# Weight sums of the second layer on GpSimd, earlier in the program; high parts of weights in two operations

## The chip, the cores and the metric

The kernel runs on one core of a Trainium2 chip. The metric is the device time of one execution in microseconds (us). Engines are called as in the profile: PE (TensorE, matmuls), PEld (its weight loads), DVE (VectorE), ACT (ScalarE), POOL (GpSimd), SP (SyncE, which here issues the large DMAs). A name with a q behind it (DVEq) is an engine's queue of instructions, where it takes branches and waits on semaphores. L832 is line 832 of the kernel before.

## The reference, cut to what matters

A Nyström attention is followed by two mixture-of-experts layers with one expert for each token. The second layer, in which all of the change lies, is this:

```python
logits = x @ w_gate + modality_bias[modality_id]
e_idx = np.argmax(logits, axis=1)
...
for e in range(E):                      # E = 8
    mask = e_idx == e
    if not mask.any():
        continue
    h = np.maximum(x[mask] @ w1[e], 0.0)          # 512 -> 1024
    out[mask] = gate_w[mask, None] * (h @ w2[e])  # 1024 -> 512
```

There are 4608 tokens. All is float32 outside; inside, a matrix is split into a float16 high part and a float16 rest, and a product is three float16 matmuls.

## The kernel before

The attention runs over 8 batches in an order written out by hand, with the first tiles of the first layer in its gaps. Then come three stretches: a loop over the first layer's tiles of 128 tokens; three tiles that stand outside of any loop (called "last", "out1" and "out2" by their plans, and first, second and third tile below); and a loop over the second layer in which one step handles two tiles of 128 tokens (`pair`). With the given inputs that loop has 17 steps. What is said of steps below counts them from 1 at the loop's start.

**A step.** Matmuls of `w1` first (L1402, 96 of them), then seven products with `w2` (L1429, 84 matmuls). The seven products are Strassen's scheme in Winograd's form: sums of blocks of the activations (`s`, on DVE, L1358 to L1370), and sums of blocks of `w2`. The sums of `w2` depend on the weights alone and are made once for each half of an expert's `w2`: `mix` (L825) writes four differences of 128x512 float32 into `tf`; `mix_hi` (L836, ACT) writes their float16 high part `wth`; `mix_lo` (L841, DVE, two operations) writes the rest `wtl`. So the chain for one half is four operations on `tf`, one on ACT, two on DVE.

**New weights.** While one expert is computed, the next expert's weights arrive in four pieces and are split: `split_hi` (L813, ACT) makes the high part `whi`, `split_lo` and `split_lo2` (L818, DVE) the rest `wlo`. A number in a table, `word`, says for a step whether a piece is split (`word > 7`) and whether it is a piece of `w2`, so that its sums are made too (`word > 11`). Each such part stands in an `If` on `word` in the step's code; it is taken in 4 of the 17 steps, and the sums in two of these, steps 7 and 8.

**What sets the order.** Each engine works through its own queue in the order in which the code issues. Where the parts of a step stand is set by a table, `PLANS`: a number is the matmul group behind which the parts are issued (for `pair`, 0 to 7 are the groups of `w1`, 8 to 14 the seven products; -1 is the head of the step). In `pair` of before, `s0` is `split_hi`, `s1` and `s2` are the two halves of the rest, `s3` is the four sums and `mix_hi`, `s4` is `mix_lo`. `f0` and `f1` (L1355) and `g0` and `g1` (L1364) make the activations' sums; ACT's `sh` of L1367 in `g1` is what the third product's later matmuls read. `u1` to `u4`, `y22`, `y21` and `y12` add the products.

**The three tiles.** They make the sums of the first expert of the second layer: the first tile those of one half (`mixa`, `mix0` to `mix2`), the third tile those of the other (`mixb`, `mix3` to `mix5`), from `again`, a second copy of that half of `w2`, which lies in the buffer `s` of the activations' sums. While the second tile runs, DVE also works out the table of the loop (`tile_table`, some 90 tiny operations, L903 to L1033) in two parts: the first stands ahead of the second tile's operations in DVE's queue, the second ahead of the third tile's. From that table SP reads which rows of tokens to load for the loop's first step (`xab`, L1084, two transposing DMAs).

**The loop's entry.** PE's first matmul of the loop waits for both of these loads, and for DVE and ACT to have come to the loop. SP's first issue of a step is the load of the next weights' piece into `stg` (L791); in step 1 it, too, waits until DVE has come to the loop.

## Time and profile before

| | |
|---|---|
| median of 3 runs | 1017.72 us (1017.53 to 1018.48) |
| profiled execution | 1013.91 us, span of its instructions 1012.2 us |
| PE busy | 964.6 us, 95% of the span |
| DVE, ACT, POOL busy | 720.7, 426.0, 228.8 us (71%, 42%, 23%) |
| mean granted TensorE clock | 0.984 |
| chain that ended last | its last 2 us: output rows (L1244, L1253) |

The profiled execution and the timed runs are different executions; the profiled one has 3.8 us less than the median. PE is busy nearly throughout, so a stretch is read by PE's idle time in it and by what ended that idle time. A matmul's row covers its latency too: in the loop each starts some 0.11 us behind the one before it and is shown as 0.27 us, so that a stall shows shorter than it is. The length of a step is best taken from one step's first matmul of L1402 to the next step's.

### The profile page before, as it was taken

To read this page: it belongs to the slowest core of one execution; us is meant where nothing else is said; L and a number is where in the kernel's file an instruction comes from. 1 tells how busy PE (TensorE), PEld (TensorE's weight loads), DVE (VectorE), ACT (ScalarE), POOL (GpSimd) and SP (SyncE) were. 2 spreads that over 40 slices of the span, in tenths; PEclk is the share of its full clock that TensorE was granted. 3 is DMA by queue.
4 is the path that set the end of the run, shared out by engine and by line. 5 is a ranking of instruction groups with operands and counts; after the bars stand their busy time and mean duration, and the time that the engine had idled before them with its cause. 6 is when DMAs were issued, how large, how long until landed. Compare 5 with 4: busy or idle time off the path is not lost. (4 is left out here: it accounts for less than half of the span.)

```text
span 1012.2 us, 36241 instructions
## 1 busy us (share of the span) xinstructions
PE 964.6 (95%) x11663; PEld 737.2 (73%) x11664; DVE 720.7 (71%) x2708; ACT 426.0 (42%) x993; POOL 228.8 (23%) x311
## 2 busy tenths in 40 slices
PE   6989998989899999999999999989999999999997
PEld 3655554656677777777767767768888888888886
DVE  6888878958777877877877777855466676545644
ACT  3565756832233433433433433333343444333332
POOL 6476766445010010010010010111100110010011
PEclk9998979989999999999999999999999999999999
DMA  8557587265565462265562345531212121221212
GB/s 281 192 184 257 181 280 291 75 226 142 117 167 157 126 183 65 66 166 156 131 183 66 72 127 148 129 98 34 63 42 63 43 59 48 61 59 46 63 44 62
DMA packets 166419, 125.31 MB, mean 124 GB/s; under 512 B 137662, under 2 KB 137662, under 8 KB 165328
## 3 DMA queue, kind: packets, MB, share of 16 engines
q1 hardware_dynamic: 155536, 95.42, 35.8%
q0 software_dynamic: 9088, 28.95, 7.5%
q8 instruction: 41, 0.67, 0.3%
q10 hardware_dynamic: 1728, 0.06, 0.1%
q14 instruction: 26, 0.21, 0.1%
HBM read 60.48 MB, written 34.83 MB: 94 GB/s over the span
## 5 line engine op out<-in xcount | busy, mean ns | idle before, releaser
L1285 PE MATMUL b_hp<-xl,whi 128*128 128x128 f16 x2368 | 204.1, 219 | 1.2 <-DMA xl<-reg 1.2
L1285 PE MATMUL b_hp<-xl,wlo 128*128 128x128 f16 x1184 | 201.9, 219 | 0.0
L1285 PEld LDWEIGHTS <-whi 128*128 128x128 f16 x2624 | 199.7, 98 | 2.6 <-issue 1.6
L1402 PE MATMUL b_hp<-xab,whi 128*128 128x256 f16 x1088 | 179.1, 273 | 1.2 <-DVEq L1453 1.2
L1402 PE MATMUL b_hp<-xab,wlo 128*128 128x256 f16 x544 | 148.3, 273 | 0.0
L1285 PEld LDWEIGHTS <-wlo 128*128 128x128 f16 x1312 | 128.5, 98 | 0.1
L1336 PE MATMUL ybank<-wlo,hh 128*128 128x512 f16 x328 | 124.6, 380 | 1.0 <-DVE wlo L809 1.0
L1336 PE MATMUL ybank<-whi,hh 128*128 128x512 f16 x328 | 124.6, 380 | 0.0
L1336 PE MATMUL ybank<-whi,hl 128*128 128x512 f16 x328 | 122.3, 380 | 0.0
L1223 POOL DMA_INDIRECT reg<-rows,si x38 | 37.4, 985 | 359.6 <-DVE rr L1154 338.5
L1402 PEld LDWEIGHTS <-whi 128*128 128x128 f16 x1088 | 106.3, 98 | 14.0 <-ACTq L1453 1.7
L1146 ACT ACTIVATE rt<-ybank,sc 128x512 f16<-128x512 f32 x38 | 26.1, 687 | 211.5 <-DVE off L1568 193.9
L1336 PEld LDWEIGHTS <-hh 128*128 128x128 f16 x656 | 62.1, 98 | 67.0 <-issue 0.5
L818 DVE SCALAR_TENSOR_TENSOR wlo<-stg,whi x76 | 92.7, 1220 | 20.3 <-issue 10.9
L1244 POOL DMA_INDIRECT out_dram<-osbb,tokb x18 | 18.5, 1030 | 294.4 <-DVEq L1517 213.4
L813 ACT ACTIVATE whi<-stg x38 | 72.3, 1903 | 0.0
L1358 DVE SCALAR_TENSOR_TENSOR s<-b_hp,r 128x256 f32<-128x256 f32 x34 | 14.4, 424 | 78.5 <-ACT r L1357 69.2
L1130 DVE TENSOR_REDUCE sc<-ybank 128x1 f32<-128x512 f32 x38 | 26.3, 691 | 56.6 <-PE L1285 49.4
L1293 ACT ACTIVATE hh<-b_hp 128x512 f16<-128x512 f32 x74 | 44.1, 597 | 48.1 <-PE b_hp L1285 28.3
L1336 PEld LDWEIGHTS <-hl 128*128 128x128 f16 x328 | 32.1, 98 | 40.1 <-issue 1.6
L1429 PEld LDWEIGHTS <-sh 128*128 128x128 f16 x544 | 53.0, 98 | 9.8 <-ACT sh L1367 3.8
L1402 PEld LDWEIGHTS <-wlo 128*128 128x128 f16 x544 | 53.2, 98 | 6.2
(437 smaller groups left out, 2149.7 us busy)
## 6 DMA issues: line engine op xcount, KB each, us to landing
stg<-in_wall_dram SPq DMA_DIRECT2D x29, 1024.0 KB, 5.5
kq<-in_qk_dram SPq DMA_DIRECT2D x32, 576.0 KB, 6.2
v<-in_v_dram SPq DMA_DIRECT2D x8, 1024.0 KB, 8.2
reg<-zrow SPq DMA_DIRECT2D x18, 264.0 KB, 8.6
v<-in_v_dram SPq DMA_DIRECT2D x8, 128.0 KB, 8.2
s<-in_wall_dram SPq DMA_DIRECT2D x1, 1024.0 KB, 6.7
xl<-reg SPq DMA_TRANSPOSE x41, 3.3
mt<-reg SPq DMA_DIRECT2D x41, 8.0 KB, 4.3
```

Of the source, the lines that this page charges most:

```text
L813: return self.tc.nc.scalar.activation(self.slot(self.ws[d].hi, i), self.slot(self.stg, i), AF.Copy, scale=WS)
L818: return self.tc.nc.vector.scalar_tensor_tensor(self.slot(w.lo, i, a), self.slot(self.stg, i, a), WS, self.slot(w.hi, i, a), op0=ALU.mult, ...
L1130: v.tensor_reduce(sc[:, 0:1], y, axis=AX.X, op=ALU.max, apply_absolute_value=True)
L1146: a.activation(rt[:, 0:DM], y, AF.Copy, scale=sc[:, 1:2])
L1223: w = nc.gpsimd.indirect_dma_start(out=k.reg[:, :], out_offset=bass.IndirectOffsetOnAxis(ap=self.si.bitcast(U32), axis=0), in_=rows, in_of ...
L1244: return nc.gpsimd.indirect_dma_start(out=self.out[:, :], out_offset=bass.IndirectOffsetOnAxis(ap=tok.bitcast(U32), axis=0), in_=osb, in_o ...
L1285: mm = nc.tensor.matmul(hp[ft // 4][:, ft % 4], lhsT=ww[c][:, ft * P:(ft + 1) * P], rhs=self.xl[:, x], start=n == 0, stop=n == 11)
L1293: self.read[i] = [nc.scalar.activation(hh[:, 4 * i:4 * i + 4], hp[i], AF.Relu)]
L1336: nc.tensor.matmul(self.y, lhsT=a[:, ft], rhs=ww[ft], start=n == 0, stop=n == 23)
L1358: v.scalar_tensor_tensor(s[:, 2, c], h[:, :, 0], 0.0, r21[:, c], op0=ALU.max, op1=ALU.subtract)
L1402: nc.tensor.matmul(hp[ft // 2][:, ft % 2], lhsT=ww[c][:, ft * P:(ft + 1) * P], rhs=self.xab[:, x], start=n == 0, stop=n == 11)
L1429: nc.tensor.matmul(bank[:, half[0]], lhsT=l[:, c], rhs=r[c], start=new and c == 0 and i == 0, stop=c == 3 and i == 2, skip_group_check=not ...
```

## The change

All sums but those of `mixa` (first tile) go from DVE to POOL. In a step they move from `s3` (behind the third product) to a part of their own, `add`, at the head of the step, behind the first group of `w1`; `s3` keeps `mix_hi`. Outside of the loop, `mixb` and `mix3` move from the third tile to the second, and `mix4` and `mix5` into the third tile's groups of `w1`. `split_hi` of the second layer becomes two operations of half the size, the second of which (`hi2`) stands three groups later. POOL reads `word` too, so that every `If` on it is now a branch for POOL as well; `add` and `hi2` are two more of them for ACT and DVE.

```diff
-    def split_hi(self, d, i):
-        return self.tc.nc.scalar.activation(self.slot(self.ws[d].hi, i), self.slot(self.stg, i), AF.Copy, scale=WS)
+    def split_hi(self, d, i, a=slice(0, 2)):
+        return self.tc.nc.scalar.activation(self.slot(self.ws[d].hi, i, a), self.slot(self.stg, i, a), AF.Copy, scale=WS)
...
-    def mix(self, v, k):
+    def mix(self, v, k, eng=None):
...
-        return self.tc.nc.vector.tensor_tensor(o, x, y, op=ALU.subtract)
+        return (eng or self.tc.nc.vector).tensor_tensor(o, x, y, op=ALU.subtract)
...
-    "out1": {-1: "out load", 3: "hh0 hl0", 7: "after1 hh1 hl1", 9: "told"},
-    "out2": {-1: "out load", 3: "hh0 hl0", 7: "after1 hh1 hl1 told", 9: "mixb mix3 mix4 mix5", 15: "rest"},
-    "pair": {-1: "out load", 0: "s0", 1: "f0 s1", 3: "f1", 5: "g0", 7: "after1 g1 s2 told", 8: "u1",
+    "out1": {-1: "out load", 3: "hh0 hl0", 7: "after1 hh1 hl1", 9: "told mixb mix3"},
+    "out2": {-1: "out load", 3: "hh0 hl0 mix4", 7: "after1 hh1 hl1 told mix5", 15: "rest"},
+    "pair": {-1: "out load", 0: "s0 add", 1: "f0 s1", 3: "f1 hi2", 5: "g0", 7: "after1 g1 s2 told", 8: "u1",
              10: "u2 u3 s3", 11: "y22 u4", 12: "y21 outb", 13: "y12 s4"},
...
-                word = field(i, CUT, 15, (ET.Activation, ET.DVE))
+                word = field(i, CUT, 15, (ET.Activation, ET.DVE, ET.Pool))
...
+                if layer:
+                    hi = [lambda d, i, a=a: wts.split_hi(d, i, a) for a in range(2)]
+                    return [part(f) for f in (*hi, wts.split_lo, wts.split_lo2)]
                 return [part(f) for f in (wts.split_hi, wts.split_lo, wts.split_lo2)]
...
-                        r = wts.mix(wts.slot(wts.stg, cut), n)
+                        r = wts.mix(wts.slot(wts.stg, cut), n, nc.gpsimd)
...
-                return dict(s0=when(7, hi), s1=when(7, lo), s2=when(7, lo2), s3=when(11, m["mixa"], m["mix0"]),
+                return dict(s0=when(7, hi), s1=when(7, lo), hi2=when(7, hi2), s2=when(7, lo2), add=when(11, m["mixa"]), s3=when(11, m["mix0"]),
                             s4=when(11, m["mix1"], m["mix2"]))
...
-        def add(v):
+        def add(v, eng=None):
             for i in range(4):
-                wts.mix(v, i)
+                wts.mix(v, i, eng)
...
-                   mix2=lambda: wts.mix_lo(p, 1, 1), mixb=lambda: add(again), mix3=lambda: wts.mix_hi(p, 0),
+                   mix2=lambda: wts.mix_lo(p, 1, 1), mixb=lambda: add(again, nc.gpsimd), mix3=lambda: wts.mix_hi(p, 0),
```

The second tile on POOL, before: the rows of output (L1244) in each of the two arms that the tile has for the two sets of weights, and nothing else.

```order
L1750 COMPARE_AND_BRANCH
L1244 DMA out_dram<-osb,tok 4608x512
L1750 UNCONDITIONAL_BRANCH
L1244 DMA out_dram<-osb,tok 4608x512
L1750 UNCONDITIONAL_BRANCH
L847 TENSOR_LOAD numi
```

The same place of the changed kernel (its lines from 1488 on have numbers up to 3 higher):

```order
L1753 COMPARE_AND_BRANCH
L1244 DMA out_dram<-osb,tok 4608x512
L832 TENSOR_TENSOR tf<-s 128x512 x2
L832 TENSOR_TENSOR tf<-s,tf 128x512
L832 TENSOR_TENSOR tf<-tf,s 128x512
L1753 UNCONDITIONAL_BRANCH
```

The four sums stand directly behind the output rows of the first tile, so POOL can start them while DVE works on the table's first part. The third tile on DVE, before, in one arm: the rests of the hidden layer (`hl`), then the four sums and the two operations of `wtl`.

```order
L1296 SCALAR_TENSOR_TENSOR hl<-b_hp_4929,hh 128x512
L1296 SCALAR_TENSOR_TENSOR hl<-b_hp_4930,hh 128x512
L1237 TENSOR_SCALAR mul<-mt 128x1
L1238 COPY tok<-mt 128x1
L832 TENSOR_TENSOR tf<-s 128x512 x2
L832 TENSOR_TENSOR tf<-s,tf 128x512
L832 TENSOR_TENSOR tf<-tf,s 128x512
L841 SCALAR_TENSOR_TENSOR wtl_4906<-tf,wth_4905 128x1024 x2
```

And now:

```order
L1296 SCALAR_TENSOR_TENSOR hl<-b_hp_4929,hh 128x512
L841 SCALAR_TENSOR_TENSOR wtl_4906<-tf,wth_4905 128x1024
L1296 SCALAR_TENSOR_TENSOR hl<-b_hp_4930,hh 128x512
L1237 TENSOR_SCALAR mul<-mt 128x1
L1238 COPY tok<-mt 128x1
L841 SCALAR_TENSOR_TENSOR wtl_4906<-tf,wth_4905 128x1024
```

The sums are gone, and the two operations of `wtl` stand behind one `hl` each. The head of a step on POOL in the changed kernel (register operations of the last two sums left out): the two issues of output rows, the `If` of `s0`, which is empty for POOL, and that of `add`.

```order
L1244 DMA out_dram<-osbb,tokb 4608x512
L1244 REGISTER_ALU
L1244 DMA out_dram<-osb,tok 4608x512
L1520 COMPARE_AND_BRANCH
L1520 UNCONDITIONAL_BRANCH x2
L1520 COMPARE_AND_BRANCH
...
L832 TENSOR_TENSOR tf<-stg 128x512
...
L832 TENSOR_TENSOR tf<-stg,tf 128x512
...
L832 TENSOR_TENSOR tf<-tf,stg 128x512
```

Before, POOL had only the two issues there, and no compare: the sums stood on DVE behind `u3`.

## Rows read from the trace of the kernel before

**Rows 1.** Timeline of PE: first matmul rows of steps 1, 2, 8, 9, 10, 11.

```profile
665.96 0.38 PE L1402 MATMUL b_hp<-xab,whi 128*128 128x256 f16 x2 [1.21 <-DVEq L1453]
688.17 0.38 PE L1402 MATMUL b_hp<-xab,whi 128*128 128x256 f16 x2
806.07 0.38 PE L1402 MATMUL b_hp<-xab,whi 128*128 128x256 f16 x2
826.73 0.38 PE L1402 MATMUL b_hp<-xab,whi 128*128 128x256 f16 x2
847.89 0.38 PE L1402 MATMUL b_hp<-xab,whi 128*128 128x256 f16 x2
867.54 0.38 PE L1402 MATMUL b_hp<-xab,whi 128*128 128x256 f16 x2
```

**Rows 2.** Timeline of PE, step 9: the stalled matmul.

```profile
841.70 0.28 PE L1429 MATMUL b_hp<-wth,sh 128*128 128x256 f16 x1 [1.05 <-ACT sh L1367]
```

**Rows 3.** Timeline of DVE and ACT, steps 7 and 8.

```profile
797.80 0.40 ACT L1367 CAST sh<-s 128x256 f16<-128x256 f32 x1 [1.18 <-DVE s L1366]
802.76 1.29 DVE L832 TENSOR_TENSOR tf<-stg 128x512 f32 x2 [0.20 <-issue]
807.75 2.55 DVE L841 SCALAR_TENSOR_TENSOR wtl<-tf,wth 128x1024 f32 x2 [0.98 <-ACT wth L836]
812.19 0.42 DVE L1358 SCALAR_TENSOR_TENSOR s<-b_hp,r 128x256 f32<-128x256 f32 x1 [1.88 <-ACT r L1357]
```

**Rows 4.** Timeline of DVE, SP, ACT, third tile and step 1; landing of L791's load.

```profile
665.62 2.36 DVE L841 SCALAR_TENSOR_TENSOR wtl<-tf,wth 128x1024 f16<-128x1024 f32 x2 [1.97 <-ACT wth L836]
666.08 0.43 SPq L791 DMA_DIRECT2D stg<-in_wall_dram  x1
673.31 0.38 ACT L1357 ACTIVATE r<-b_hp 128x256 f32<-128x256 f32 x1 [5.47 <-PE L1402]
674.78 0.42 DVE L1358 SCALAR_TENSOR_TENSOR s<-b_hp,r 128x256 f32<-128x256 f32 x1 [6.80 <-issue]
stg<-in_wall_dram SPq DMA_DIRECT2D x1, 1024.0 KB, 6.8
```

**Rows 5.** Groups of POOL by line and shape: count, busy us, mean ns.

```profile
L368 POOL TENSOR_TENSOR lh<-kq 128x288 f32<-128x288 f32 x64 | 46.7, 742 | 13.7 <-DVE kq L376 6.8 <-DMA kq<-in_qk_dram 5.5 <-DVE ql L376 0.7
L430 POOL TENSOR_TENSOR a<-a,am 128x576 f32<-128x576 f32 x16 | 18.6, 1163 | 13.5 <-DVE am L428 11.4 <-DVE r_pm L267 1.1 <-DVE ru L550 0.8
```

**Rows 6.** POOL and DVE in the attention; line 292's durations (minimum, median, maximum).

```profile
119.20 0.74 POOL L368 TENSOR_TENSOR lh<-kq 128x288 f32<-128x288 f32 x1
119.23 0.74 DVE L292 TENSOR_SCALAR r_gs<-r_gs 128x5 f32<-128x5 f32 x1
L292 DVE TENSOR_SCALAR r_gs<-r_gs x8: 158/458/756, 63.5 to 233.6; 128x5 f32<-128x5 f32 x8
```

**Rows 7.** Timeline of POOL, DVE, PE and SP, first to third tile; landing of L1084's DMAs.

```profile
646.33 0.98 POOL L1244 DMA_INDIRECT out_dram<-osb,tok  x1 [0.30 <-DVE wtl L841]
647.87 0.16 DVE L911 SCALAR_TENSOR_TENSOR tab_act<-tab_key,tab_c 128x8 f32<-128x8 f32 x1
650.00 1.28 DVE L1296 SCALAR_TENSOR_TENSOR hl<-b_hp,hh 128x512 f16<-128x512 f32 x2
652.32 1.89 PE L1336 MATMUL ybank<-whi,hl 128*128 128x512 f16 x8
657.96 3.14 SPq L1084 DMA_TRANSPOSE xab<-reg  x2
DMA to landing us min/median/max: 3.2/3.4/5.0
```

**Rows 8.** Timeline of PE; two stretches with the granted clock (column behind POOL's).

```profile
214.78 0.61 PE L634 MATMUL pair<-wb,at 64*128 64x144 f32 x2 [2.85 <-DVE at L447]
214.48:221.31 6.83, 6.43 (x40) 4.59 (x41) 2.14 (x7) 2.30 (x5) 0.83 (x4) 0.50 0.67 276
67.71:71.12 3.41, 3.41 (x48) 1.38 (x46) 1.77 (x9) 1.07 (x3) 1.70 (x2) 0.50 0.46 149
```

More of the change, by code (lines that the diff above doesn't have):

```diff
@@ L1511, in spots @@
             def spots(p):
-                hi, lo, lo2 = early(p)
+                hi, hi2, lo, lo2 = early(p)
                 m = mix(p)
```

## Prediction

> **What bounds the kernel now.** I read the page first: PE is busy 95% of the span at a mean granted clock of 0.984, so an edit to DVE, ACT or POOL can gain only where PE waits for them. Then PE's timeline. From one step's first matmul to the next, an ordinary step of the loop takes 19.65 us (867.54 - 847.89); step 1 takes 22.21, step 8 20.66 and step 9 21.16 [rows 1]. The excess is 2.56 + 1.01 + 1.51 = 5.08 us. Another 1.21 us of idle stands before the loop's first matmul. That is all that this change can reach: 6.3 us, 0.6% of the time.
>
> Steps 8 and 9 are the steps behind those in which the sums of `w2` are made. PE's wait in step 9 ends with ACT's `sh` of L1367 [rows 2]. The same chain a step earlier shows why: the sums begin on DVE at 802.76, the two operations of `wtl` end only at 810.30, four microseconds into step 8, and the first `s` of that step comes at 812.19, 6.1 us behind the step's start, after a further 1.88 us of waiting for ACT's `r` [rows 3]. In step 7 the `sh` of L1367 was done at 798.2 and no stall is seen there. ACT's `wth` stands between sums and `wtl`, so ACT too arrives late in step 8.
>
> Step 1 is another matter. DVE's first `s` comes at 674.78, 8.8 us behind the step's start, after 6.80 us in which the profile shows nothing to wait for; ACT's `r` comes at 673.31 after 5.47 us [rows 4]. Both wake just behind the landing of the 1 MB load that SP issued at 666.08 and that took 6.8 us, to 672.88. I read this as instructions of the step that arrive behind that load.
>
> **The change, part by part.** *Sums on POOL, their price.* No 128x512 subtract runs on POOL before. Nearest are 742 ns for 288 elements and 1163 ns for 576 [rows 5]; scaled to 512 that is 1.03 to 1.32 us. I take 1.2, so 4.8 us for four, with 4.1 to 5.3 as bounds; on DVE they took 4 x 0.65 to 0.69 = 2.7 us. The Trainium skill, GPSIMD Engine Reference, section 3.1, gives 4497 ns for a sum of 2048 float32, by which 512 would be an estimated 1.12 us, 4.5 us for the four.
>
> *Sums in the loop.* They leave DVE's tail in steps 7 and 8 for POOL at the head of these steps. Before, they began at 802.76, 16.3 us into step 7 (its start is 806.07 - 19.65 = 786.4); on POOL they are done some 6 us into it, 10 us before DVE began them. `mix_hi` stays behind the third product, so POOL's slower work is covered by that time; without the cover it would cost 2.1 us a step (4.8 - 2.7). `wth` no longer waits for sums, `wtl` no longer reaches into the next step, and `s` and `r` of steps 8 and 9 come when they do in others: 1.01 + 1.51 = -2.52 us. Bounds: 0 to -2.52; I take it all, since what is late there has lost both of its causes.
>
> *What POOL's sums do to DVE.* In the attention, a 128x5 operation of DVE that starts at 119.23 beside a POOL sum of 119.20 to 119.94 ends at 119.97, 0.74 us, where the shortest of its eight takes 0.158 [rows 6]. So some DVE operations stand still until POOL's running sum is over, then one gets through. In the loop's heads the first operations of DVE (`s` and `al`) read PSUM and one SBUF tile; only `sl` and `wlo` read two SBUF tiles. And that step has slack: `sh` in step 9 was needed about 2 us later than step 7 delivered it. I take +0.2 us for steps 7 and 8 together; bounds 0 and 2 x 2.2 (a hold of 4.2 us each, as worked out below, less 2.0 of slack).
>
> The Trainium skill, SBUF — State Buffer, section "SBUF: two separate sides", speaks against the change here: an operation of DVE with two SBUF inputs and one of GpSimd that reads SBUF share a pair of ports under an exclusive lock, and the later one waits for the whole of the other. The 0.74 us above agrees with a wait for the end, though that operation is one with a single tile read.
>
> *`mixb` in the second tile.* This is what the change costs. POOL's queue there holds the output rows, 646.33 to 647.31, and then the four sums at once. DVE is at that time in the table's first part, tiny operations such as L911, most with two SBUF inputs, back to back until `hl` at 650.00, 1.28 us for two [rows 7]. The sums would run from 647.4 to 652.2. If one tiny operation gets through for each sum, DVE does 4 x 0.16 = 0.6 us of its work in 4.8 and is held for D = 4.2 us (bounds: 0, and 4.8). The first `hl` is then done at 650.00 + 0.68 + 4.2 = 654.9, and PE, which started its first product with `hl` at 652.32, does so 2.6 us later.
>
> PE then loses a little more, if the clock falls. Before, PE's idle of 2.85 us ahead of 214.78 was followed by 6.83 us at a granted clock of 0.50 (1.2 instead of 2.4 GHz), and another stretch at 0.50 lasted 3.41 us [rows 8]. 2.6 is near to 2.85, so I let the clock fall. I take the short stretch: 3.41 us at half clock, 1.7 us of work lost, with 0 and 3.4 as bounds. PE ends the third tile at 664.75 (665.96 less 1.21), so now at 664.75 + 2.6 + 1.7 = 669.05.
>
> Beside it the table: its second part stands behind the held one, so SP issues the loads of `xab` 4.2 us later, at 662.2 instead of 657.96 with the second about 1.9 later; with 3.2 to 5.0 us to land they are there at 667.3 to 669.1. DVE, freed of sums (2.7 us) in the third tile and with `wtl` ahead of its wait, is no longer what opens the loop. So step 1 starts at about 669.3, that is +3.35 us, and the 1.21 us of idle are already in that sum. Without the clock's fall it is 667.6 to 669.1: +1.65 to +3.1.
>
> *Step 1.* DVE comes to the loop earlier against PE, and its instructions no longer queue behind the load. But ACT's stand where they stood, behind its first rows of output, and SP's load comes some 4 us later too. If ACT still wakes 7.2 us behind the load, DVE's `s` can gain only what it trailed ACT's `r` by (674.78 - 673.69 = 1.1), less 0.7 by which the load is later against the entry: -0.4. If ACT's instructions pass ahead of the load: all of 2.56. The rows are equally near to both; I take the middle, -1.4.
>
> *The rest, at nothing.* `hi` in two halves: one more operation on ACT, at most 0.4 us (a 128x256 `r` takes 0.38 [rows 4]), and ACT is busy 42%; it lets `r` past half a `hi` sooner, and is covered by that idle time. More `If`s: branches on ACT and DVE, whose queues mostly wait for PE; an ordinary step has five of them and PE still sets its 19.65. `word` read on POOL: one load of a register, where POOL only waits for output rows; without that cover the price is bounded by an issue of output rows, 0.98 us a step. `mix4` and `mix5` behind `hl` in the third tile: two operations of 1.2 us where the sums of 2.7 were, covered by what is taken away.
>
> *Sum:* 3.35 - 1.4 - 2.52 + 0.2 = -0.4 us. The profiled execution of before took 1013.91, span 1012.2; so 1013.5 by its measure. The median of the runs is 3.8 above it, 1017.72, and I carry the difference over: 1017.3 us.
>
> **Rivals.** A is this case: -0.4, between -1.6 (ACT's instructions pass: -2.56) and +0.6 (they don't: -0.4); 0.50.
> B, the clock holds or falls only briefly, and the loads land early: entry +1.65, and as SP's load is then 2.3 us behind the entry, ACT's instructions pass: 1.65 - 2.56 - 2.52 + 0.2 = -3.2, 1014.5 us. For it: the loads' median of 3.4; against it: 2.6 us of idle. 0.21.
> C, DVE isn't held in the second tile, because the 128x5 case doesn't carry over: entry -1.0 (the idle that DVE's arrival made), step 1 -0.4, steps 8 and 9 -2.52, so -3.9, 1013.8 us. 0.08.
> D ends on the other side: the hold bites in the loop's heads. `sl` of each head waits for up to four sums; with `sh`'s chain 4.2 us late and 2.0 of slack, steps 7 and 8 stall 2.2 us each: -0.4 - 0.2 + 4.4 = +3.8, 1021.5 us. It decides from about 3.3 us of hold per head. For it: heads are where DVE has the `s` chain; against it: most operands there are in PSUM. A clock stretch of 6.83 us in the second tile would add 1.7 to it or to A's upper end. 0.15 together.
> E, the sums are early but steps 8 and 9 stall half as before, because ACT's `hi` and rows of output are what made `r` late: -0.4 + 1.3 = +0.9, 1018.6 us. 0.06.
>
> **How the numbers follow.** A change under 0.2%, 2.0 us, can't be told from none. A and E lie within it: 0.56. B and C are faster: 0.29. D is slower: 0.15. The likeliest is A, 1017.3, its own range 1016.1 to 1018.3. The range over the cases reaches from C, 1013.7, to 1020.2; above it lies most of D.
>
> **What would show it.** Right: POOL's four sums beside stretched tiny operations of DVE behind 647, the first product with `hl` of the second tile some 2.6 us late and a stretch at 0.50 behind it; the loop's start 3.35 us later; steps 8 and 9 of 19.65; step 1 between 19.65 and 21.8. Wrong: table operations at 0.15 to 0.23 us beside POOL's sums (C), steps 7 or 8 of more than 20 (D), or `s` of step 8 still at 6 us behind its start (E). The forecast as a whole falls if the sums on POOL take 2 us each, since then every hold doubles.

## The result and the profile after

The changed kernel takes 1029.83 us, median of 7 runs (1027.61 to 1033.24), against 1020.53 us for the kernel before, median of 7 runs that took turns with it or stand in the table above (1017.53 to 1025.63). The ratio is 1.0093 with an interval of 1.0071 to 1.0115: slower by 7 to 12 us. The forecast was 1017.3, no change that can be told. All ratios here compare runs in the usual state; among the runs of e1's chip, two of e1 (1111.05 and 3336.33 us) and one of before (3334.62) are outside of it and left out.

The profiled execution took 1028.70 us, and its page says:

```profile
span 1022.9 us, 36658 instructions
PE 963.8 (94%) x11663; PEld 734.0 (72%) x11664; DVE 723.6 (71%) x2696; ACT 426.7 (42%) x997; POOL 243.5 (24%) x323
```

Two things stand in these numbers already. POOL has 14.7 us more work (243.5 against 228.8): its twelve sums take 16.3 us by their rows, and the rest of its work is a little shorter. And time less span is 5.8 us, where it was 1.7 us before (1013.91 - 1012.2). So 4 us are lost where no instruction is recorded.

**The second tile.** Timeline of POOL and DVE of the changed kernel, from the second tile on (start, duration, then in brackets the idle time ahead and what ended it):

```profile
651.99 0.97 POOL L1244 DMA_INDIRECT out_dram<-osb,tok  x1 [0.30 <-DVE wtl L841]
652.98 2.51 POOL L832 TENSOR_TENSOR tf<-s 128x512 f32<-128x512 f32 x2
655.43 1.28 POOL L832 TENSOR_TENSOR tf<-s,tf 128x512 f32<-128x512 f32 x1
656.79 1.29 POOL L832 TENSOR_TENSOR tf<-tf,s 128x512 f32<-128x512 f32 x1
...
652.40 4.35 DVE L1742 TENSOR_SCALAR start<-one,took 128x8 f32<-128x8 f32 x1
656.78 0.17 DVE L1743 TENSOR_TENSOR start<-start,ebase 128x8 f32<-128x8 f32 x1
656.87 1.23 DVE L1744 TENSOR_TENSOR tooki<-took,base 128x1 int32<-128x1 f32 x1
```

These three lines of DVE are the second to fourth operation of the table's preparation, which starts at 652.21. The first of the three had this row in the profile of before:

```profile
646.74 0.23 DVE L1739 TENSOR_SCALAR start<-one,took 128x8 f32<-128x8 f32 x1
```

In the changed kernel it ends at 656.75, just behind the third sum (655.43 + 1.28 = 656.71). One operation then fits in ahead of the fourth sum, and the next ends at 658.10, just behind that (658.08). DVE is at `hl` 8.64 us behind the preparation's start (660.85 - 652.21) where it was 3.45 us before (650.00 - 646.55): held by 5.2 us. By the rows, the hold begins a little ahead of the sums: the operation starts 0.58 us ahead of the first sum's row and would have ended before it; the profile's times on POOL are rough. PE's timeline, from the second tile's first matmul:

```profile
648.97 0.17 PE L1740 MATMUL b_z<-sl 128*128 128x16 f16 x1 [0.61 <-issue]
661.59 2.85 PE L1336 MATMUL ybank<-whi,hl 128*128 128x512 f16 x8 [3.50 <-DVE hl L1296]
675.97 0.39 PE L1402 MATMUL b_hp<-xab,whi 128*128 128x256 f16 x2 [0.28 <-ACTq L1453]
```

And the windows view of the stretch behind its wait (granted clock behind POOL's column):

```profile
662.43:665.84 3.41, 3.41 (x21) 2.22 (x20) 3.03 (x29) 0.69 (x1) 0.00 (x0) 0.50 0.05 7
```

Eight matmuls in 2.85 us instead of 1.89 [rows 7]: the clock fell to its half (1.2 GHz) for 3.41 us behind an idle time of 3.50. From the second tile's first matmul to the loop's start PE takes 27.0 us, where it took 22.64 before (to 665.96 [rows 1]) from this row:

```profile
643.32 0.17 PE L1737 MATMUL b_z<-sl 128*128 128x16 f16 x1 [0.61 <-issue]
```

At the entry it waits 0.28 us and not 1.21 [rows 1].

**The loop.** The same rows of PE as [rows 1] (steps 2, 8, 9, 10), and the two stalls of step 8:

```profile
697.62 0.38 PE L1402 MATMUL b_hp<-xab,whi 128*128 128x256 f16 x2
815.52 0.38 PE L1402 MATMUL b_hp<-xab,whi 128*128 128x256 f16 x2
827.18 0.28 PE L1429 MATMUL ybank<-whi,ah 128*128 128x256 f16 x1 [0.36 <-ACT ah L1359]
831.63 0.28 PE L1429 MATMUL b_hp<-wth,sh 128*128 128x256 f16 x1 [1.42 <-ACT sh L1367]
837.82 0.38 PE L1402 MATMUL b_hp<-xab,whi 128*128 128x256 f16 x2
857.47 0.38 PE L1402 MATMUL b_hp<-xab,whi 128*128 128x256 f16 x2
```

Step 1 takes 21.65 us, step 8 22.30, step 9 19.65: together 0.4 us less than before. Step 9's stall [rows 2] is gone, and step 8 has a larger one. Timeline of POOL and DVE in the head of step 8, which starts at 815.52:

```profile
819.16 0.97 POOL L1244 DMA_INDIRECT out_dram<-osb,tok  x1 [1.43 <-ACT osb L1254]
820.15 2.50 POOL L832 TENSOR_TENSOR tf<-stg 128x512 f32 x2
822.60 1.26 POOL L832 TENSOR_TENSOR tf<-stg,tf 128x512 f32<-128x512 f32 x1
824.02 1.26 POOL L832 TENSOR_TENSOR tf<-tf,stg 128x512 f32<-128x512 f32 x1 [0.15 <-POOL tf L832]
...
815.46 2.58 DVE L841 SCALAR_TENSOR_TENSOR wtl<-tf,wth 128x1024 f32 x2 [0.24 <-issue]
820.40 0.42 DVE L1358 SCALAR_TENSOR_TENSOR s<-b_hp,r 128x256 f32<-128x256 f32 x1 [2.37 <-issue]
821.62 2.54 DVE L1353 TENSOR_TENSOR sl<-s,sh 128x256 f16<-128x256 f32 x1
824.08 2.28 DVE L818 SCALAR_TENSOR_TENSOR wlo<-stg,whi  x1
826.29 0.41 DVE L1358 SCALAR_TENSOR_TENSOR s<-b_hp,r 128x256 f32<-128x256 f32 x1
```

`sl` takes 0.41 us elsewhere and `wlo` 1.23; here they take 2.54 and 2.28. `sl` ends just behind the gap between the third and the fourth sum (823.86 to 824.02), and `wlo` 1.1 us behind the fourth (825.28). The sums meet them because POOL's second issue of output rows, which stands ahead of the sums, waits for ACT's `osb`: they begin 4.6 us into the step, where DVE's first `s` comes 4.9 us into it. The second `s` comes 10.8 us into the step. In step 7 the sums begin 3.2 us and the first `s` comes 3.4 us into the step; `sl` takes 1.41 us and `wlo` 2.28 there, and PE does not stall. DVE's `s` has one operand in PSUM, and takes its usual 0.41 us beside the sums.

**The end.** From the last step's start to the span's end it takes 27.9 us, before 26.8. The last matmuls come as before; ACT's last rows (L1253) start 1.4 us behind the end of the last matmul instead of 0.8, and from the end of POOL's last issue to the span's end it takes 3.8 us instead of 3.2. And behind the span's end at 1022.9 instructions are still loaded. DMA view of the stretch 1024 to 1030 (forty equal slices, then packets by queue):

```profile
DMA  0000000000032140000000000000000000000000
q14 instruction: 4, 0.03, 1.7%
q8 instruction: 1, 0.02, 1.0%
```

In the trace of before there is no packet in the same stretch behind its end.

### The profile page after: what moved, and what is told of

Read it like the earlier page. It is cut to its first block, busy times and chain, and to the rows that moved or that the text cites. A ratio compares the mean times of both kernels' runs of the same rounds, so it can differ in the third digit from the quotient of the medians.

```text
span 1022.9 us, 36658 instructions
## 1 busy us (share of the span) xinstructions
PE 963.8 (94%) x11663; PEld 734.0 (72%) x11664; DVE 723.6 (71%) x2696; ACT 426.7 (42%) x997; POOL 243.5 (24%) x323
## 5 line engine op out<-in xcount | busy, mean ns | idle before, releaser
L818 DVE SCALAR_TENSOR_TENSOR wlo<-stg,whi x76 | 94.9, 1249 | 19.8 <-issue 10.4
L1244 POOL DMA_INDIRECT out_dram<-osbb,tokb x18 | 17.5, 973 | 281.1 <-DVEq L1520 227.8
L1296 DVE SCALAR_TENSOR_TENSOR hl<-b_hp,hh 128x512 f16<-128x512 f32 x74 | 50.8, 688 | 17.6 <-ACT hh L1293 17.6
```

The lines of the kernel that those rows point to most:

```text
L818: return self.tc.nc.vector.scalar_tensor_tensor(self.slot(w.lo, i, a), self.slot(self.stg, i, a), WS, self.slot(w.hi, i, a), op0=ALU.mult, ...
L1244: return nc.gpsimd.indirect_dma_start(out=self.out[:, :], out_offset=bass.IndirectOffsetOnAxis(ap=tok.bitcast(U32), axis=0), in_=osb, in_o ...
L1296: self.read[i].append(nc.vector.scalar_tensor_tensor(hl[:, 4 * i:4 * i + 4], hp[i], 0.0, hh[:, 4 * i:4 * i + 4], op0=ALU.max, op1=ALU.subt ...
```

## The experiments

The theory held after reading the trace: **POOL's sums hold DVE**, in the second tile and in the heads of the loop's steps. The rival: **the program as a whole** has become slower, since the profiled run took longer ahead of the change as well (5.4 us from PE's first matmul to the second tile, 642.4 against 637.0), though no instruction in that stretch has changed, and 4 us lie outside the span. Each group of runs had its own chip and its own runs of before. The stretches in the table are from PE's timeline: from the second tile's first matmul (L1737 before, L1740 in the others) to the loop's start, the loop's steps, the last step's start to the span's end; a dash is an ordinary 19.65. The ratio is from the timed runs; the other columns are from one profiled execution each, and step 1 in particular scatters (see at e5).

| run | ratio to before (interval) | 2nd tile to loop | step 1 | 7 | 8 | 9 | end | time less span | instructions |
|---|---|---|---|---|---|---|---|---|---|
| before | | 22.64 | 22.21 | - | 20.66 | 21.16 | 26.8 | 1.7 | 36241 |
| changed | 1.0093 (1.0071 to 1.0115) | 27.00 | 21.65 | - | 22.30 | - | 27.9 | 5.8 | 36658 |
| e1 | 0.9984 (0.9956 to 1.0011) | 22.59 | 22.78 | - | 20.09 | - | 27.3 | 1.7 | 36607 |
| e2 | 1.0034 (1.0008 to 1.0060) | 28.02 | 21.49 | - | 20.30 | 20.89 | 26.8 | 1.7 | 36394 |
| e3 | 0.9996 (0.9973 to 1.0019) | 22.59 | 22.33 | - | 20.30 | 20.98 | 26.7 | 1.7 | 36341 |
| e4 | one run | 22.67 | 21.54 | - | 20.30 | 20.99 | 26.7 | 1.7 | 36350 |
| e5 | 0.9991 (0.9972 to 1.0009) | 22.59 | 23.05 | - | 19.84 | - | 27.4 | 1.7 | 36622 |
| e6 | 1.0011 (0.9992 to 1.0030) | 21.73 | 22.11 | - | 20.13 | 20.07 | 27.4 | 5.9 | 36674 |
| e7 | 1.0102 (1.0084 to 1.0121) | 27.01 | 22.12 | - | 22.33 | - | 27.9 | 5.0 | 36658 |
| e8 | one run | 25.19 | 21.07 | - | 20.30 | 20.88 | 26.7 | 1.7 | 36345 |
| e10 | 1.0057 (1.0036 to 1.0079) | 26.96 | 22.03 | 20.81 | 22.24 | - | 27.8 | 1.8 | 36537 |
| e13 | 0.9981 (0.9964 to 0.9999) | 21.67 | 21.80 | - | 19.76 | - | 27.4 | 1.7 | 36628 |

**e1, the third tile back.** The changed kernel, with both lines of the three tiles and `mixb`'s engine as before:

```diff
-    "out1": {... 9: "told mixb mix3"},
-    "out2": {... 3: "hh0 hl0 mix4", 7: "after1 hh1 hl1 told mix5", 15: "rest"},
+    "out1": {... 9: "told"},
+    "out2": {... 3: "hh0 hl0", 7: "after1 hh1 hl1 told", 9: "mixb mix3 mix4 mix5", 15: "rest"},
-    mixb=lambda: add(again, nc.gpsimd)
+    mixb=lambda: add(again)
```

> The loop as changed; the sums of mixb back on DVE in the third tile, as before. Held theory (DVE's operations with two SBUF tiles stand still until POOL's train of sums has a gap): DVE's first part of the table is 3.5 us again instead of 8.6, the first hl product of the second tile doesn't wait, and from the second tile's first matmul to the loop's start PE takes 22.6 us instead of the 26.85 of the changed kernel. Step 8 stays at about 22.3 and step 9 at 19.65. Time: 4 to 5 us under the changed kernel, 0 to +0.5 us against the loop before, so within 0.2% of before if the attention takes as long. Rival theory (the program as a whole got slower, since the attention of the profiled run took 4.7 us longer although its code is the same): the attention is again 4 to 5 us longer than in the profile of before, and the time is 4 to 6 us above before.

The second tile is as before. The stretch ahead of it takes 631.5 us here, less than in the profile of before: it differs between chips and executions, and that part of the rival fell. Step 8 missed: 20.09 and not 22.3. The same sums meet the same operations there; DVE timeline of e1, where POOL's third sum starts at 807.47:

```profile
807.25 0.54 DVE L1353 TENSOR_TENSOR sl<-s,sh 128x256 f16<-128x256 f32 x1
807.98 2.02 DVE L818 SCALAR_TENSOR_TENSOR wlo<-stg,whi  x1 [0.18 <-issue]
```

`sl` came 0.3 us ahead of the second sum's end and got in before the third went on (1.44 us instead of 1.26); in the changed kernel it came 0.8 us earlier against the sums, and stood through the rest of the second and the whole of the third. What a meeting costs depends on tenths of a microsecond. e14 (below) shows it again: it executes e1's instructions and one more, its `sl` comes 6.05 us into step 8 and not 5.89, and the step takes 20.99 us where e1 and its other variants take 20.09 to 20.11. DVE timeline of e14:

```profile
814.61 1.28 DVE L1353 TENSOR_TENSOR sl<-s,sh 128x256 f16<-128x256 f32 x1
815.82 2.28 DVE L818 SCALAR_TENSOR_TENSOR wlo<-stg,whi  x1
```

**e2, the loop back.** The three tiles as changed; `add` taken out of the loop, its sums back in `s3` on DVE, `word` on ACT and DVE alone.

> The second and third tile as changed; the sums of the loop back on DVE behind the third product. Held theory: second tile to loop 26.85 us as in the changed kernel, steps 8 and 9 at 20.66 and 21.16 as before, step 1 at 21.65, so about 3.6 us above before by these parts. Rival theory (program as a whole): 8 to 10 us above before, with 4 to 5 of them in the attention. If the held theory is wrong and the table was late for another reason, such as the load of the rows, the first part of the table does not show single operations of 1 to 4 us beside POOL's sums.

Slower by 0.34%: the second tile alone makes the kernel slower (the halves of `split_hi`, which e2 has too, do not: e3). DVE is held 4.26 us in one operation, PE waits 3.52 us, and this time the half clock lasted 6.83 us instead of 3.41; the entry is 1.0 us later than in the changed kernel. The longer stretch doesn't belong to e2: e15 (below), which executes the changed kernel's instructions, had it too, and took 28.10 us to the loop. Windows view of e15, granted clock behind POOL's column:

```profile
665.27:672.10 6.83, 5.73 (x30) 3.50 (x31) 6.21 (x49) 0.69 (x1) 0.58 (x1) 0.50 0.13 43
```

**e3, the halves alone.** The kernel before with `split_hi` in two operations.

> The kernel before with the high parts of the second layer's weights in two operations, and nothing else. Held theory: no difference from before, within 1 us in every stretch; steps 1, 8 and 9 at 22.2, 20.7 and 21.2. Rival (the attention changes with any change to the program): the attention differs by some us from before's profile though no instruction in it differs, up or down.

No difference in time. Steps 8 and 9 are 0.54 us shorter together, since ACT comes to `r` 0.9 us earlier in step 8 (4.57 us into it instead of 5.48): a gain that the prediction put at nothing.

**e4, POOL busy with writing.** e3, and in the second tile:

```diff
-    "out1": {... 9: "told"},
+    "out1": {... 9: "told idle"},
+    idle=lambda: [nc.gpsimd.memset(moe.osbb, 0.0) for _ in range(9)]
```

> The kernel of the two halves, with nine memsets of 128x512 on POOL (they only write) in the second tile where the changed kernel has its four sums, about 5 us of POOL work; the sums stay on DVE. They are extra work that computes nothing. Held theory in its narrow form (what holds DVE is POOL reading SBUF): the table's operations beside the memsets take their usual 0.15 to 0.23 us and the second tile is as before. Rival (any POOL work at that place holds DVE, or PE's wait has another cause): single operations of 1 to 5 us beside the memsets and a late hl, as in the changed kernel.

Timeline of POOL and DVE:

```profile
647.93 5.21 POOL L1731 MEMSET osbb<- 128x512 f32 x9
...
647.38 0.56 DVE L1742 TENSOR_SCALAR start<-one,took 128x8 f32<-128x8 f32 x1
649.16 0.17 DVE L913 TENSOR_TENSOR tab_key<-tab_key,eidx 128x8 f32<-128x8 f32 x1
649.24 0.43 DVE L915 TENSOR_SCALAR tab_act<-tab_act 128x8 f32<-128x8 f32 x1
650.80 0.61 DVE L934 CAST numi<-tab_num 128x2 int32<-128x2 f32 x1
```

And DVE in the profile of before:

```profile
648.06 0.17 DVE L913 TENSOR_TENSOR tab_key<-tab_key,eidx 128x8 f32<-128x8 f32 x1
648.15 0.16 DVE L915 TENSOR_SCALAR tab_act<-tab_act 128x8 f32<-128x8 f32 x1
649.44 0.17 DVE L934 CAST numi<-tab_num 128x2 int32<-128x2 f32 x1
```

L1742 takes 0.56 us at the head of 5.2 us of memsets (it ends at 647.94, where their row begins) and 4.35 beside the sums; the table's first part is 1.0 us longer, not 5.2, and PE doesn't wait. So it is not POOL's being busy that holds DVE for long. The narrow form of the theory didn't hold either: some operations did wait, by up to 0.44 us each. The Trainium skill, SBUF — State Buffer, section "Who interferes with whom", says that an operation of DVE with two SBUF inputs contends only with a GpSimd operation that reads, and that TENSOR_SCALAR, copies and casts can enter a two-port mode in which they contend with any. The trace agrees: what was held beside the memsets is TENSOR_SCALAR, COPY and CAST (L915 0.43 us instead of 0.16, L934 0.61 instead of 0.17), or stood right behind such a one in the queue, while L913, a TENSOR_TENSOR with two SBUF inputs, took its usual 0.17.

**e8, two sums of four.** e2, with `mixb`'s first two sums on POOL in the second tile and the other two on DVE in the third.

> The loop as before; of the four sums of mixb the first two on POOL in the second tile, the other two on DVE in the third. Held theory (DVE stands still as long as POOL's train runs): a hold of some 2.5 us instead of 5.2, hl some 2.5 us late, PE's wait there 1.0 to 1.5 us instead of 3.5, no stretch at half clock behind it; second tile to loop 23.5 to 25.5 us. Rival (a fixed cost of starting POOL's operations there): the same wait as with four.

Timeline of POOL, DVE and PE:

```profile
653.59 2.50 POOL L832 TENSOR_TENSOR tf<-s 128x512 f32<-128x512 f32 x2
...
653.07 3.06 DVE L1742 TENSOR_SCALAR start<-one,took 128x8 f32<-128x8 f32 x1
...
659.90 1.90 PE L1336 MATMUL ybank<-whi,hl 128*128 128x512 f16 x8 [1.21 <-DVE hl L1296]
...
674.77 0.38 PE L1402 MATMUL b_hp<-xab,whi 128*128 128x256 f16 x2 [2.43 <-DMA xab<-reg]
```

The hold goes with the sums' length: 2.8 us (3.06 less 0.23) for 2.5 us of sums, and PE's wait falls from 3.50 to 1.21. No fall of the clock. PE is then early and waits 2.43 us for the loads of `xab`, which are late with the table: here the second price of the hold is seen by itself. Step 1 of e8 shows one thing more, in SP's and ACT's timelines:

```profile
677.50 0.01 SPq L791 DMA_DIRECT2D stg<-in_wall_dram  x1
677.75 0.38 ACT L1357 ACTIVATE r<-b_hp 128x256 f32<-128x256 f32 x1 [2.31 <-PE L1402]
```

SP issued the 1 MB load 2.7 us behind the step's start, and ACT's first `r` came 3.0 us behind it, not 7.35 as in before: with a late load ACT did pass ahead of it. The step took 21.07 us with a wait of 1.26 us for ACT's queue ahead of step 2.

**e5, the sums first.** e1 with the sums ahead of the output rows in POOL's queue:

```diff
-    "pair": {-1: "out load", 0: "s0 add", ...
+    "pair": {-1: "add out load", 0: "s0", ...
```

> The third tile as before, and in the loop POOL's sums ahead of the step's two issues of output rows instead of behind them, so that in steps 7 and 8 they run while DVE still has nothing with two SBUF tiles to do. Held theory (what costs is that the sums meet sl and wlo): POOL's sums start at 0.1 to 3 us behind a step's start instead of 4.8, in step 8 only when wtl of step 7 has read tf; sl takes 0.41 us in step 7, is held by less than 1 us in step 8; steps 8 and 9 together at most 40.0 us where the version with the sums behind the rows has 39.74 and before 41.82, and the time is 1 to 3 us below before. Rival (an engine loses time to the sums wherever they stand, or output rows that go out later hold their buffers): step 7, 8 or 9 longer than 20.5, time not below before.

Steps 8 and 9 take 39.49 us, 2.33 less than before, most of the 2.52 forecast, though `wlo` still stands 2.06 us beside the last sums in step 8. Step 1 was 0.84 us longer than in before, so the time did not fall by what can be told. That is not the doing of the sums' new place: e1 and the five variants of it below, which have them behind the rows, take 22.45 to 23.18 us in step 1, as e5 does with 23.05. The four profiles of the changed kernel's instructions (changed, e7, e15, e17) have 21.48 to 22.12.

**e6, all early.** e5, with the sums of `mixb` on DVE at the third tile's head and `wtl` behind the third product:

```diff
-    "out2": {-1: "out load", ... 9: "mixb mix3 mix4 mix5", 15: "rest"},
+    "out2": {-1: "out load mixb", ... 8: "mix3 mix4 mix5", 15: "rest"},
-             10: "u2 u3 s3", 11: "y22 u4", 12: "y21 outb", 13: "y12 s4"},
+             10: "u2 u3 s3 s4", 11: "y22 u4", 12: "y21 outb", 13: "y12"},
```

> As e5, and wtl made behind the third product too (at once after wth), and the sums of mixb on DVE at the head of the third tile, ahead of its hl, with wth behind the first group of products. Held theory: tf is free by the end of step 7, so the sums of step 8 start within 1 us of its start and steps 8 and 9 take 19.65 each; the loop's entry loses its wait for DVE (1.2 us), so second tile to loop 21.4 to 21.9 us. Time 3 to 5 us below before. Rival: DVE's sums at the third tile's head make its first hl late, and PE waits there instead, or wtl ahead of y22 makes the next step's banks late: second tile to loop above 22.6, steps 8 or 9 above 20.

The entry gained 0.9 us as expected; steps 8 and 9 lost 0.7 against e5, so `wtl` is better left where it was. The time did not follow the span, whose median is 2.2 us below that of before on the chip: time less span is 4.9 to 7.0 us in its twelve runs, and 1.7 to 1.8 in the 23 of before.

**e7, the changed kernel again.**

> The changed kernel once more, unaltered, on the chip of the other versions. Held theory: 5.4 us above before by the stretches (second tile to loop +4.4, loop -0.4 to +0.2, end of the program +0.6 to +1.2), so a ratio of 1.0045 to 1.0065, and the attention no longer than in the profiles of the other versions. Rival (the attention of the changed kernel is longer by itself): ratio near 1.009 again, and an attention 4 us above those of the other versions of this chip.

Ratio 1.0102. The stretches came out as before, and the rival's figure for the time as well, but not by the stretch ahead of the second tile, which was 644.9 us where e5, e6 and e8 on this chip had 641.9 to 645.1: the remainder is outside the span (4.8 to 7.6 us in its runs).

**e9, e14 to e19, what lies outside the span.** The first thought was program size. e9 adds one-column copies on ACT to e1, in the arm of the second tile that these inputs don't take, so that nothing more is executed; e14 does so with memsets on POOL, e18 with ACT and DVE, e19 with DVE. e15 and e16 leave four of 44 dummy matmuls out of an arm not taken in the changed kernel and in e6; e17 adds three memsets on DVE to such an arm of the changed kernel. By the traces' counts e14, e17, e18 and e19 execute one instruction more than the version they add to, the others none.

```diff
+            if n == 1:
+                for _ in range(2):
+                    nc.scalar.copy(moe.osbb[:, 0:1], moe.osbb[:, 1:2])
```

> Of the changed kernel some 4 us were outside the span of its instructions: time less span is 5.0 to 5.8 us in its runs and in those of the version with everything early, and 1.7 in all others. The compiled program of ACT is 61504 bytes in these two and at most 61312 in the others, 61440 being 15 times 4096. This run is the version with the third tile as before (61312 bytes), with two copies of one column on ACT in the arm of the second tile that these inputs don't take, so that nothing more is executed: 61440 bytes. Theory (the size of ACT's program past 61440 bytes costs a fixed time outside the span): time less span 1.7, time as the version without them. Rival (it is something else in those two): 1.7 as well, so the next run tells them apart.

> As the run before with three such copies, none of them executed: ACT's program has 61504 bytes, the size in the changed kernel. Theory (size): time less span 5.0 to 5.8, time some 4 us above the run with two copies, the span the same within its scatter. Rival (not ACT's size): time less span 1.7.

> Some 3.5 to 4 us of the changed kernel's time lie outside its instructions' span, and ACT's program size was not the cause. What is left that the two slow versions share: the five engines' compiled programs have 932608 bytes together in both; in all the others at most 932352. This run is the version with the third tile as before (932160 bytes), with eight one-column memsets on POOL in the arm of the second tile that isn't taken: 932736 bytes, none of the added ones executed. Theory (the sum of the programs past a bound between 932352 and 932608): time less span 5 to 5.8, time some 4 us above before. Rival (something that both versions execute): 1.7, time within 0.2% of before.

> The changed kernel with four of the 44 dummy matmuls left out of the arm of the third tile that isn't taken, so that nothing less is executed: 932096 bytes. Theory (sum of the programs): time less span 1.7, time 5 to 6 us above before instead of 9 to 10, ratio 1.005 to 1.0065. Rival: time less span 5 and more, ratio 1.009 to 1.010.

> The version with everything early, with the same four matmuls left out of the arm not taken: 932096 bytes. Theory: time less span 1.7, time some 4 us under the same version with them, ratio to before 0.997 to 0.9985. Rival: time less span 5 and more, ratio 1.000 to 1.002.

> The 3.5 to 4 us outside the span show in the trace as a burst of five instruction packets, one for each engine's stream, that lands 2.8 to 3.3 us behind the last instruction; kernels with 1.7 us have none or a single one there. The sum of the sizes is not the cause. What is left by sizes: DVE's program is 105664 and 106176 bytes in the two kernels with the burst (both 192 over a multiple of 512), 105920 and others elsewhere. This run is the changed kernel with three one-column memsets on DVE in the arm not taken: 105920 bytes. Theory (how DVE's program ends in its blocks): no burst, time less span 1.7. Rival (what the kernels execute near the end, not sizes): burst as before, 5 to 5.8.

> The version with three ACT copies in the arm not taken, and three memsets on DVE there: each of the five programs then has exactly the size of the version with everything early (ACT 61504, DVE 106176, PE 684608, POOL 44672, SP 35648), none of the added ones executed. Theory (sizes): burst, time less span 5 to 5.8. Rival (what is executed, or where in the program things stand): no burst, 1.7.

> As the run before without ACT's copies: DVE 106176, ACT 61312. Theory in the form that DVE's size alone decides: burst, 5 to 5.8. In the form that ACT's and DVE's sizes together decide, and by the rival: no burst, 1.7.

Every form of the theory fell. Time less span stayed 1.7 in e9 (both), e14, e18 and e19, and 4.9 to 7.2 in e15, e16 and e17; the ratios are 0.9988 (0.9968 to 1.0007), 0.9997 (0.9974 to 1.0019), 0.9999 (0.9981 to 1.0016), 1.0006 (0.9981 to 1.0032) and 0.9990 (0.9963 to 1.0017) for the first five, and 1.0098 (1.0067 to 1.0129), 1.0031 (1.0014 to 1.0047) and 1.0074 (1.0032 to 1.0116) for the others. e18 has all five program sizes of e6 and none of its 4 us. DMA view of e18 from 1021 to 1027, as far behind its span (1019.9) as the view above:

```profile
DMA packets 0, 0.00 MB, mean 0 GB/s; under 512 B 0, under 2 KB 0, under 8 KB 0
```

What these runs leave is what is executed, and there the kept traces say more than the totals in the table. Counted over a whole trace, with register operations and branches, ACT executes 2999 instructions in each of the six profiles with the loss (changed, e6, e7, e15, e16, e17) and at most 2981 in every other. No other engine's count separates them: DVE has 5345 to 5349 in the six and 5315 to 5380 in the others, POOL 1451 or 1463 in the six and 1463 in e5 too. This is a coincidence of two things in the traces, not a cause that a run has shown.

**e10, the high part whole.** The changed kernel with `split_hi` in one operation and no `hi2`.

> The changed kernel with the high parts of weights in one operation again; ACT's program shrinks to 59584 bytes. Theory (size, and the lock in second tile and step 8): time less span 1.7, span as in the changed kernel (second tile to loop 27.0, loop 319 to 320, end 27.9): time 5 to 6 us above before, some 4 us under the changed kernel; step 8 at most 0.6 us longer. Rival (not the size): time less span 5 and more, 9 to 10 us above before.

Ratio 1.0057, and time less span 1.7 to 1.8: 4 us are won back, though the loop is 1.5 us longer (step 7 stalls as well, 20.81, as it did in e15 with 20.86 and not in the changed kernel, whose instructions e15 shares). What remains, some 5.8 us, is about what the trace shows: second tile 4.3, loop 1.0, end 1.0. That `split_hi` stands in two operations does not by itself cost the 4 us either: e1, e3 and e5 have it so, at 1.7.

**e13, what gained.** e5 with `mixb` on DVE at the third tile's head, `mix3` to `mix5` one group earlier, and the second half of the high part in the `If` of `s1`.

> The parts that gained, together: in the loop POOL's sums ahead of the output rows, wtl where it was; mixb on DVE at the head of the third tile; the second half of the high part in the If of the first rest, which keeps ACT's program at 60864 bytes. Held theory: second tile to loop 21.7 (before 22.64), steps 8 and 9 together 39.5 to 39.8 (41.82), step 1 at 22 to 23 (22.2), end of the program 27.4 (26.8), time less span 1.7: time 1.5 to 3 us below before, ratio 0.997 to 0.9985. Rival (the hi half in step's first If is late again for ACT, or step 1 loses what is gained): not below before.

Ratio 0.9981 (0.9964 to 0.9999): just faster than before, and faster than the changed kernel by 1.1% as the two ratios stand. Of the versions run, this is the only one that can be told to be faster than before; by the stretches its entry gained 1.0 us, step 1 0.4 and steps 8 and 9 2.4, and its end lost 0.6. The same with the loop's sums on DVE was not run.

## Why the prediction was wrong

- **The sum** was -0.4 us, measured +9.3. By the stretches of the profile: entry +4.4 (27.00 - 22.64), step 1 -0.56, steps 8 and 9 +0.13, end +1.1, outside the span +4.1 (5.8 - 1.7). That is 9.1. Against the terms of the prediction the entry is 1.0 us more, step 1 0.8, steps 8 and 9 2.45, the end 1.1 and what lies outside the span 4.1. The two largest are the two steps that failed: that the heads of the loop's steps have the slack for POOL's sums, and that time less span stays what it was. Apart from the change, before itself has a median of 1020.53 in seven runs and not the 1017.72 of three that the forecast stood on; this moves the time in us and not the difference.
- **The hold in the second tile** was seen: its place, PE's late `hl`, the fall of the clock, the late table. Its size was short: 5.2 us and not 4.2, since four sums took 5.1 us and not 4.8, and one operation of DVE stood through three sums; "then one gets through" for each sum was wrong: only the gap ahead of the fourth sum let one through. PE waited 3.5 us instead of 2.6. The entry came 4.4 us late instead of 3.35. e2 shows this part by itself, and e8 that it goes with the sums' length.
- **The clock**: the short stretch of 3.41 us at half speed came, as forecast. Which of the two comes is luck: e2, and e15 with the changed kernel's instructions, got 6.83.
- **Step 1** gained 0.56 (0.09 to 0.73 over the four profiles of these instructions), near the lower of the two bounds of the case A (0.4 and 2.56), not the middle of 1.4. Timelines of SP and ACT:

```profile
676.12 0.43 SPq L791 DMA_DIRECT2D stg<-in_wall_dram  x1
683.73 0.38 ACT L1357 ACTIVATE r<-b_hp 128x256 f32<-128x256 f32 x1 [4.84 <-PE L1402]
```

ACT's `r` came 7.6 us behind the load: ACT did not pass ahead of it. The load was not later against the entry, as the prediction had it by 0.7 us, but came 0.15 us behind the step's start (0.12 before). In e8 it was 2.7 us late, and ACT passed, as the prediction's other bound and its rival B assume; that the instructions queue behind the load fits all this and was not tested by itself.
- **Steps 8 and 9** were the step that failed in the loop. Their old stalls went, as said; but "the hold bites in the loop's heads" (rival D, 0.15) came true in step 8, where `sl` and `wlo` lost 3.2 us. The working put 0.2 us there because "that step has slack", and had the sums done "some 6 us into it"; they were done 9.3 us into step 7 and 9.8 into step 8, since they start behind output rows that wait for ACT, and so they met the `s` chain. Step 7 did have the slack: `sl` and `wlo` lost 2.05 us there without a stall. Step 8 has less of it: it starts with `wtl` of step 7, which the change left at the end of the step, so its `s` chain is already late (first `s` 4.9 us into the step, 3.4 in step 7). e5 shows that the 2.52 us were there to be had: 2.33 with the sums moved ahead of the rows.
- **The end of the program** was in no term. `word` on POOL was put at nothing, covered by POOL's idle time; e1, e5 and e13 carry POOL's `If`s, and their end is some 0.6 us longer than that of e2, e3, e4 and e8, which have none. The other half microsecond comes with POOL's sums in both places (changed, e7, e10, e15, e17) and lies behind POOL's last issue of rows; its cause stays open.
- **Outside the span** lie 3.5 to 4 us that no term and no rival held. Carrying the 3.8 us between median and profile over to the changed kernel took for granted that time less span doesn't change. What triggers the late loads of instructions, and whether they are what the time is spent on, stays open: it is neither the sizes of the programs (e14 to e19) nor ACT's alone (e9). The runs with the loss executed 36658 to 36674 instructions, those without it 36628 or fewer, and of ACT's own count it is 2999 against 2981 or fewer; e10 lost it with 121 instructions fewer, 79 of them ACT's. That is a lead and was not tried.
- **The stretch ahead of the second tile** wasn't a cause: with the same instructions it took 630 to 647 us over the profiles of all these runs, and 637 to 647 over the five of before and of the changed kernel's instructions.

## What to carry to other kernels

Work moved to GpSimd can be paid by VectorE where the two meet: before moving it, list what VectorE does in the same microseconds, which of it works on SBUF alone (here `s` and `al`, with an operand in PSUM, were not held), and reckon with the whole train of GpSimd's operations as the hold of the first such operation that meets it. Ask also what stands ahead of the moved work in its new queue: it starts when that is done, not at the place where the code issues it. Here the move paid in the loop where POOL's queue was free before DVE started (e5, the sums ahead of the output rows), and not beside a chain that the matmuls wait for. Compare time less span in both kernels too: a loss there is in no timeline.

## What the runs showed of the hardware that was not expected

- A single 128x8 operation of DVE stood 4.35 us beside three sums of POOL that followed one another without a gap, and went on in the 0.08 us ahead of the fourth (656.71 to 656.79), which had to wait for the third's result.
- POOL is held as well: a sum that takes 1.26 us alone took 2.06 in step 7 of the changed kernel (803.13) and 2.25 in that of e1 (787.73) while `wlo` ran.
- 128x512 sums on POOL take 1.26 to 1.29 us each when nothing holds them; the prediction took 1.2, and the estimate that it worked out from the Trainium skill, GPSIMD Engine Reference, section 3.1, was 1.12.
- In the runs whose time less span is 4.8 to 7.6 us instead of 1.7, the profiled execution shows five instruction loads that land 2.8 to 3.3 us behind the last recorded instruction.
- Nine memsets on POOL, 5.2 us without a gap, held single operations of DVE (TENSOR_SCALAR, COPY, CAST) by at most 0.44 us, where 5.1 us of sums held one through three of them.
